# A finer table for placing masks, sums, reciprocals and products in the output stages of an attention and GEGLU kernel

## The chip, the cores and the metric

One core of a Trainium2 chip runs the whole program. The metric is the device time of one execution in microseconds, given as the median of several runs.

## What is computed

Sliding-window attention over 8 batches, 8 heads, 576 positions and 64 dimensions, then a feed-forward block with a gate. Heads 0 to 3 see the last 32 positions; heads 4 to 7 see 32 positions at distances of 4.

```python
rel = pos[:, None] - pos[None, :]
mask_plain = (rel >= 0) & (rel < 32)
mask_dil = (rel >= 0) & (rel < 128) & (rel % 4 == 0)
scores = where(masks, q @ k.T / sqrt(64), -1e9)
attn = softmax(scores)
x = (attn @ v).transpose(0, 2, 1, 3).reshape(4608, 512)
out = (gelu(x @ w_gate) * (x @ w_val)) @ w_out      # 512 -> 1536 -> 512, float32
```

## The kernel before

**Chunks and units.** The feed-forward part goes through nine chunks (`c`) of 512 tokens. The attention is cut into 32 units (`n`): a batch has four, `n // 4` is the batch; of each four the first two are plain (two heads each), the last two dilated. Unit 4b + i fills the i-th of the four tiles `xT` for batch b, which is the i-th quarter of the contraction in the first feed-forward product. A chunk of tokens so needs all units of its batches before it can finish its first products. Chunks 1 to 5 do the attention of later batches between their own feed-forward work.

**One chunk.** The entry products (`ffn1`, L533, and `ffn1_two`, L545, for the first two of the twelve column blocks) make gate and value in two PSUM banks; ScalarE takes the Gelu (L557) and VectorE multiplies (L558) into `u_all`. `ffn1_two` goes through the contraction quarter by quarter, so that the last unit's `xT` is needed only for its last four products of sixteen. Then the output products (`ffn2`, L564): four blocks of 128 tokens, twelve products each, every block stored by a copy on ScalarE (`store`, L575) and a DMA on SyncE's queue. This last part of a chunk is called its output stage.

**One attention unit.** Scores (`emit_s`, L339 plain, L369 dilated) go into the four banks `SB`; ScalarE takes the exponential into a tile `P` (L349 and L350, L371). What lies outside the window has to become zero. There are two ways. With `pe_mask` four products of the identity with a bias tile (L332 plain, L355 dilated) are put into PSUM ahead of the scores, so the exponential gives zero there. Otherwise VectorE multiplies `P` by a mask of zeros and ones (L379, called "mask" below). The list `biased` names the units that use the bias. Units 0 to 3 always do. Then `emit_pv` (L383; products at L442) makes the values ("num": P times v) and the sums ("den": P times ones). VectorE turns the sums into reciprocals with a transpose, a reciprocal and a transpose (`norm_r`: L500, L505, L507; "chain" below) and multiplies (`norm_x`: L518 plain, L521 dilated; "product" below) into `xT`. In chunks 3 to 6 some units are done during the entry products instead (`values_a`), in the scores' banks, with wider forms.

**The banks.** PSUM has eight banks. `mm0` is 0 or 4 and names the half that a chunk's feed-forward uses; `SB = 4 - mm0` is the scores' half. In the output stage of chunks 1 to 5, block 0 goes to a bank (`first`) of the last entry products, blocks 1 to 3 all go to bank `mm0`, and values and sums take the banks `V = mm0 + 1` to `mm0 + 3`. `first` is one of these. In a plain unit the values take bank V and 64 columns of the next, the sums the end of bank V + 1 and bank V + 2. The halves are swapped after chunks 1, 2 and 3.

**The order.** The program is emitted in the order of the text, and each engine keeps that order; the schedule is written by hand. In an output stage the table `places` says where what goes: "2.3s" means scores before the fourth product (number 3) of block 2, "1.12v" a unit's values after block 1, behind its store. In chunks 1 to 5 a "v" emits values, sums, the next waiting mask, the chain and the product together; in the last block the mask is left for later. One unit's scores are emitted during the last entry products of the chunk, so that its exponential can run beside block 0. The lines that the change and the prediction touch:

```python
        SB = 4 - mm0
...
        V = mm0 + 1
...
            first = pairs[(NNB - 2 + swap) % 2] + (pairs[(NNB - 2 + swap) % 2] == mm0)
```

Of the kernel before, what the change touches and what calls it, by code (L numbers as in the profile page):

```python
# [38 lines left out]
def kernel(  # L39
# [11 lines left out]
    B, H, S, D = q.shape  # L51
# [328 lines left out]

        return emit_mask

    def emit_pv(n, b0, parts=("num", "den"), wide=False):  # L383


        b, hp = n // NHP, n % 2
        vp, vd, vt, vr = tiles["v", b]
        pt = tiles["P", n]
        mms = []

        def add(hl, c0, dims, lhs, p0, pdims, st):

            base = ps[64 * hl : 64 * hl + 64, b0 + c0 // 512, c0 % 512 : c0 % 512 + 1]
            o = bass.AP(tensor=base.tensor, offset=base.offset, ap=[base.ap[0]] + dims)
            rhs = bass.AP(tensor=pt.tensor, offset=pt.offset + p0, ap=[pt.ap[0]] + pdims)
            mms.append((o, lhs, rhs, st))

        def run(n):
            return [[1, n]]

        if is_plain(n):
            if "num" in parts:
                for j in range(5):
                    for hl in range(2):
                        lhs = vp[:, j, hp, 2 * hl, :] if j < 4 else vt[:, hp, 2 * hl, :]
                        w = (PW, PW, PW, P, PT)[j]
                        add(hl, j * P, run(w), lhs, hl * PH + j * PW - (32 if j == 4 else 0), run(w), j in (0, 4))
            if "den" in parts:
                d0 = 1024 if wide else 960

                groups = (
                    ((0, 0, 4, P), (P, P, 3, 32), (PH - PT, 512, 1, PT))
                    if wide
                    else ((0, 0, 1, 64), (64, 64, 1, 64), (PW, P, 3, P), (P, P, 3, 32), (PH - PT, 512, 1, PT))
                )
                for i, (p0, q0, runs, w) in enumerate(groups):
                    for hl in range(2):
                        st = i == 0 or i == (2 if wide else 1)
                        add(hl, d0 + q0, [[P, runs], [1, w]], ones[:, 0:D], hl * PH + p0, [[PW, runs], [1, w]], st)
        else:  # L420
            if "num" in parts:
                for s in range(2):
                    for m in range(3):
                        for hl in range(2):
                            h, p0 = 2 * hp + hl, (2 * s + hl) * DW
                            if m < 2:
                                add(hl, 512 * s + m * NCL, run(P), vd[:, h, 2 * m + s, :], p0 + m * NCL, run(P), m == 0)
# [3 lines left out]
            if "den" in parts:  # L431

                groups = (
                    ((0, 0, DW, 1024), (1, 0, DW, 1536))
                    if wide
                    else ((0, 0, 192, 288), (0, 192, 96, 800), (1, 0, 96, 896), (1, 96, 192, 1312))
                )
                for i, (s, c, w, c0) in enumerate(groups):
                    for hl in range(2):
                        add(hl, c0, run(w), ones[:, 0:D], (2 * s + hl) * DW + c, run(w), wide or i != 2)  # L440
        for o, lhs, rhs, st in mms:
            nc.tensor.matmul(o, lhs, rhs, start=st, stop=True, skip_group_check=True)  # L442

# [236 lines left out]
    scores = {0: range(4, 8), 1: range(8, 12), 2: range(12, 17), 3: range(17, 22), 4: range(22, 27), 5: range(27, 32)}  # L680
    values_b = {1: range(8, 12), 2: range(12, 16), 3: range(17, 20), 4: range(22, 24), 5: range(27, 28)}
    values_a = {3: {4: 16}, 4: {2: 20, 6: 21}, 5: {1: 24, 4: 25, 7: 26}, 6: {1: 28, 4: 29, 7: 30, 10: 31}}
    biased = (6, 7, 8, 9, 10, 11, 12, 13, 14, 15)

    four = "1.5s 1.9v 1.12s 2.6v 2.12s 3.3v 3.12s 3.12v"
    three = "1.4s 1.12v 2.3s 2.12v 3.2s 3.12s 3.12v"
    two = "1.4s 1.12v 2.3s 2.12v 3.2s 3.12s"
    one = "1.4s 1.12v 2.3s 2.12s 3.6s"
    places = {1: four, 2: four, 3: three, 4: two, 5: one}
    places = {c: [(int(w[0]), int(w[2:-1]), w[-1]) for w in p.split()] for c, p in places.items()}  # L690
    late = None
    for c in range(NCH):
# [61 lines left out]
        if c == 0:  # L754
            load_batch_rest(2)
            ffn2(c, 0, 0, {5: [s_next]})
            store(c, 0, 0, "act")
            ffn2(c, 1, 1, {4: [s_next], 8: [lambda: md(4)]})
            store(c, 1, 1, "act")
            s_next()  # L760
            ffn2(c, 2, 0, {4: [lambda: md(5)], 6: [s_next], 9: [lambda: md(6)]})
            store(c, 2, 0, "act")
            ffn2(c, 3, 1, {2: [lambda: md(7), lambda: num(4, 4)], 8: [lambda: num(5, 6)]})
            store(c, 3, 1, "act")
            num(6, 2)
            num(7, 4)
        else:
            todo = list(values_b.get(c, ()))
            lone = c in values_b
            first = pairs[(NNB - 2 + swap) % 2] + (pairs[(NNB - 2 + swap) % 2] == mm0)  # L770

            def pv(last):
                n = todo.pop(0)
                emit_pv(n, V)
                if not last:
                    mask_next()
                norm(n, V)

            late = None
            mask_next()  # L780
            for tb in range(4):
                at = [(fc, kind) for t, fc, kind in places.get(c, ()) if t == tb]

                def do(kind, after):
                    if kind == "s":
                        s_next()
                        if not lone:
                            mask_next()
                    else:
                        pv(after and tb == 3)  # L790

                hooks = {}
                for fc, kind in at:
                    if fc < NNB:
                        hooks.setdefault(fc, []).append(lambda kind=kind: do(kind, False))
                bank = mm0 + tb if not lone else first if tb == 0 else mm0
                ffn2(c, tb, bank, hooks)
                store(c, tb, bank, "dve" if c > 5 and tb == 3 else "act")
                for fc, kind in at:
                    if fc == NNB:  # L800
                        do(kind, True)
            if lone:

                late = "bank"
                if len(values_b[c]) > 2:
                    mm0 = 4 - mm0
                    late = "x"
            while masks:
                mask_next()
# [28 lines left out]
```

The softmax here doesn't subtract the row's maximum and nothing guards it: scores larger than these inputs give would overflow.

## Time and profile before

| | |
|---|---|
| median of 5 runs | 362.01 us (361.17 to 362.93) |
| the profiled execution, its own time | 362.93 us |
| its span in the profile | 360.9 us |
| output stage of chunk 1: first output product to the end of the last | 91.3 to 107.2 us |
| chunk 2: first entry product, last four of `ffn1_two` | 109.0, 112.2 us |
| chunk 3: the same | 149.3, 152.5 us |
| VectorE: multiply of the Gelu (L558) | 108 of 683 ns |
| VectorE: transposes of the chain (L507) | 32 of 778 ns |
| ScalarE: table load between Gelu and exponential | 1.28 us |

The page of a profile gives busy time by engine and by groups of instructions: line, engine, operation, output and inputs with their shape, count, then busy time and mean length, then the idle time before the group and what ended it. The chain of waits gives start, length and what, in order of time, followed back from the last instruction. A timeline has start, length, engine, line and operation, and in brackets how long the engine was idle before and what released it. PE is TensorE, PEld its weight loads, DVE VectorE, ACT ScalarE, POOL GpSimd, SP SyncE. The lengths of single matmuls (380 ns at 512 columns) overlap; their distance is what counts.

### The profile page before, as it was taken

How to read it: one execution, taken by the hardware profiler on the slowest of the kernel's cores; microseconds unless marked ns; L12 is line 12 of the kernel's file. 1: busy time of each engine (PE TensorE's matmuls, PEld its weight loads, DVE VectorE, ACT ScalarE, POOL GpSimd, SP SyncE). 2: the span in 40 equal slices, each digit the busy share in tenths (PEclk: the TensorE clock that was granted, in tenths of full speed). 3: DMA queues.
4: the chain of work that ended last, by engine and by line, in shares of the span. 5: the costliest groups of instructions: out<-in, count | busy, mean ns of one | idle time of the engine just before them, and what ended most of it. 6: DMA issues, size and time to landing. Idle time of an engine off the chain costs nothing.

```text
span 360.9 us, 5997 instructions
## 1 busy us (share of the span) xinstructions
PE 344.7 (96%) x2358; PEld 166.3 (46%) x2358; DVE 196.1 (54%) x298; ACT 146.0 (40%) x212; POOL 78.2 (22%) x110
## 2 busy tenths in 40 slices
PE   5789999999989999899999999999999999999995
PEld 2554454444544445444444444544454444444442
DVE  3575446743275425765479838893679613403320
ACT  2733254253543354433663365436543223312321
POOL 2580344540431431044003410050000000000000
PEclk9959999999999999999999999999999999999999
DMA  8999999999999997599538961795100020011002
GB/s 201 235 179 211 218 142 203 176 164 238 185 130 229 181 157 126 136 170 145 112 94 187 157 96 74 181 161 84 60 29 0 13 105 2 1 61 57 0 29 87
DMA packets 107291, 45.30 MB, mean 126 GB/s; under 512 B 83040, under 2 KB 102496, under 8 KB 107264
## 3 DMA queue, kind: packets, MB, share of 16 engines
q1 hardware_dynamic: 84272, 31.21, 40.5%
q0 software_dynamic: 21456, 12.01, 26.5%
q10 hardware_dynamic: 1536, 1.70, 2.1%
q8 instruction: 18, 0.29, 0.4%
q14 instruction: 9, 0.07, 0.1%
HBM read 40.13 MB, written 9.44 MB: 137 GB/s over the span
## 4 chain that ended last, share of the span: by engine, by line
PE 79%; DMA 13%; DVE 4%; POOL 2%; ACT 1%; issue 0%; ACTq 0%; SPq 0%; POOLq 0%
PE ps L533 42%; PE ps L564 25%; PE ps L442 4%; DMA xT<-in_k_dram 3%; DMA st<-in_k_dram 3%; DMA wv<-in_moe_w_val_dram 3%; PE ps L545 3%; DMA wo<-in_moe_w_out_dram 2%; DVE xT L521 1%; PE ps L369 1%; DMA sv<-in_v_dram 1%; PE ps L339 1%; PE ps L455 1%; DVE dt L500 1%; DVE rb L507 1%; PE ps L355 1%
## 5 line engine op out<-in xcount | busy, mean ns | idle before, releaser
L558 DVE SCALAR_TENSOR_TENSOR u_all<-g,ps 128x512 f16<-128x512 f16 x108 | 72.6, 683 | 75.7 <-PE ps L533 66.0
L557 ACT ACTIVATE g<-ps 128x512 f16<-128x512 f32 x108 | 63.6, 597 | 123.5 <-PE ps L533 109.6
L564 PE MATMUL ps<-wo,u_all 128*128 128x512 f16 x432 | 101.1, 380 | 0.8 <-DMA wo<-in_moe_w_out_dram 0.4
L533 PE MATMUL ps<-xT,wg 128*128 128x512 f16 x392 | 100.6, 379 | 0.3
L533 PE MATMUL ps<-xT,wv 128*128 128x512 f16 x392 | 100.6, 379 | 0.0
L564 PEld LDWEIGHTS <-u_all 128*128 128x128 f16 x432 | 39.2, 98 | 45.1 <-issue 1.2
L533 PEld LDWEIGHTS <-wv 128*128 128x128 f16 x392 | 38.4, 98 | 46.4 <-issue 0.2
L533 PEld LDWEIGHTS <-wg 128*128 128x128 f16 x392 | 37.3, 98 | 44.6 <-issue 2.1
L575 ACT ACTIVATE osb<-ps 128x512 f32<-128x512 f32 x33 | 19.7, 597 | 48.6 <-PE ps L564 48.6
L500 DVE STREAM_TRANSPOSE dt<-ps 128x576 f32<-128x576 f32 x25 | 19.5, 779 | 26.2 <-PE ps L442 26.1
L199 POOL CAST qp<-st 128x2048 f16<-128x2048 f32 x6 | 11.4, 1893 | 100.4 <-DMA st<-in_k_dram 87.5
L507 DVE STREAM_TRANSPOSE rb<-rc 128x576 f32<-128x576 f32 x32 | 24.9, 778 | 1.1
L371 ACT ACTIVATE P<-ps 128x1152 f16<-128x1152 f32 x16 | 18.1, 1129 | 13.5 <-PE ps L369 13.5
L349 ACT ACTIVATE P<-ps 128x960 f16<-128x960 f32 x16 | 15.5, 970 | 9.5 <-PE ps L339 9.5
L521 DVE TENSOR_TENSOR xT<-ps,rb 128x576 f16<-128x576 f32 x16 | 17.8, 1122 | 0.3
L577 DVE TENSOR_SCALAR osb<-ps 128x512 f32<-128x512 f32 x3 | 2.1, 692 | 27.8 <-PE ps L564 27.8
L545 PE MATMUL ps<-xT,wg 128*128 128x512 f16 x40 | 15.8, 395 | 1.4 <-DVE xT L521 0.9
L545 PE MATMUL ps<-xT,wv 128*128 128x512 f16 x40 | 15.7, 392 | 0.0
L442 PE MATMUL ps<-P,ones 128*64 128x192 f16 (+5 forms) x174 | 11.6, 248 | 2.2 <-ACT P L371 1.0
L379 DVE TENSOR_TENSOR P<-P,mask_p 128x1344 f16<-128x1344 f16 x10 | 9.3, 938 | 6.8 <-ACT P L350 6.8
L379 DVE TENSOR_TENSOR P<-P,mask_d 128x1152 f16<-128x1152 f16 x8 | 6.1, 757 | 11.1 <-ACT P L371 11.1
L470 DVE STREAM_TRANSPOSE dt<-ps 64x576 f32<-64x576 f32 x14 | 10.9, 781 | 0.4
(83 smaller groups left out, 268.5 us busy)
## 6 DMA issues: line engine op xcount, KB each, us to landing
out_dram<-osb SPq DMA_DIRECT2D x36, 256.0 KB, 2.0
sv<-in_v_dram SPq DMA_DIRECT2D x40, 128.0 KB, 3.7
st<-in_q_dram SPq DMA_DIRECT2D x24, 128.0 KB, 3.6
st<-in_k_dram SPq DMA_DIRECT2D x24, 128.0 KB, 3.1
qd<-in_q_dram POOLq DMA_DIRECT2D x7, 256.0 KB, 4.6
qd<-in_k_dram POOLq DMA_DIRECT2D x7, 256.0 KB, 6.3
vd<-in_v_dram POOLq DMA_DIRECT2D x7, 256.0 KB, 7.3
wg<-in_moe_w_gate_dram POOLq DMA_DIRECT2D x3, 512.0 KB, 8.2
```

What stands on the lines that cost most here:

```text
L349: nc.scalar.activation(pt[:, :, 0:PB], sb[:, 0, :, 0:PB], AF.Exp, bias=0.0, scale=scale)
L371: nc.scalar.activation(pt, ps[:, b0 : b0 + 4, 0:DW], AF.Exp, bias=0.0, scale=scale)
L442: nc.tensor.matmul(o, lhs, rhs, start=st, stop=True, skip_group_check=True)
L500: nc.vector.transpose(dst, den)
L507: nc.vector.transpose(rb.rearrange("p (b c) -> p b c", c=32), bass.AP(tensor=rc.tensor, offset=rc.offset, ap=[rc.ap[0], [1, 18], [0, 32]]),)
L521: nc.vector.tensor_tensor(dst.rearrange("p (i m s) -> p i m s", m=2, s=2), num, rb.rearrange("p (s m i) -> p i m s", s=2, m=2), ALU.mult,)
L533: nc.tensor.matmul(ps[:, b0 + gi, :], w[:, kc, ns], xT[kc][:, tok], start=(kc == 0), stop=(kc == NKC - 1))
L545: nc.tensor.matmul(ps[:, pairs[nb] + gi, :], w[:, kc, ns], xT[kc][:, tok], start=(kc == 0), stop=(kc == NKC - 1),)
L557: nc.scalar.activation(g, ps[:, b0, :], AF.Gelu)
L558: nc.vector.scalar_tensor_tensor(u_all[:, nb, :], g, USCALE, ps[:, b0 + 1, :], ALU.mult, ALU.mult)
L564: nc.tensor.matmul(ps[:, bank, :], u_all[:, fc, tb * P : (tb + 1) * P], wo_t[fc // 4][:, fc % 4, :], start=(fc == 0), stop=(fc == NNB - 1),)
L575: nc.scalar.activation(osb, ps[:, bank, :], AF.Copy, bias=0.0, scale=1.0 / USCALE)
```

## The change

The table of places is rewritten with more kinds of entries: "v" emits sums, values and the chain; "x" the product; "m" a mask; "s" scores; "w" is a "v" in the scores' banks. Sums are emitted before values wherever both are emitted at once. The first unit's values of an output stage follow block 0 by two products in chunks 1 to 3. Units 8 to 15 lose the bias products and get masks on VectorE. In chunk 1 the last unit's values go to the scores' banks, and the halves of PSUM are not swapped afterwards; after chunks 2 and 3 they are.

```diff
-    def emit_pv(n, b0, parts=("num", "den"), wide=False):
+    def emit_pv(n, b0, parts=("den", "num"), wide=False):
...
-            if "num" in parts:
-                for j in range(5):
-                    for hl in range(2):
-                        lhs = vp[:, j, hp, 2 * hl, :] if j < 4 else vt[:, hp, 2 * hl, :]
-                        w = (PW, PW, PW, P, PT)[j]
-                        add(hl, j * P, run(w), lhs, hl * PH + j * PW - (32 if j == 4 else 0), run(w), j in (0, 4))
             if "den" in parts:
...
+            if "num" in parts:
+                for j in range(5):
+                    for hl in range(2):
+                        lhs = vp[:, j, hp, 2 * hl, :] if j < 4 else vt[:, hp, 2 * hl, :]
+                        w = (PW, PW, PW, P, PT)[j]
+                        add(hl, j * P, run(w), lhs, hl * PH + j * PW - (32 if j == 4 else 0), run(w), j in (0, 4))
...
-    biased = (6, 7, 8, 9, 10, 11, 12, 13, 14, 15)
-    four = "1.5s 1.9v 1.12s 2.6v 2.12s 3.3v 3.12s 3.12v"
-    three = "1.4s 1.12v 2.3s 2.12v 3.2s 3.12s 3.12v"
-    two = "1.4s 1.12v 2.3s 2.12v 3.2s 3.12s"
-    one = "1.4s 1.12v 2.3s 2.12s 3.6s"
-    places = {1: four, 2: four, 3: three, 4: two, 5: one}
+    biased = (6, 7)
+    places = {
+        1: "0.0m 1.2v 1.2x 1.2s 1.2m 1.12s 2.1v 2.1x 2.1m 2.12s 3.1v 3.1m 3.1x 3.12w 3.12x",
+        2: "0.0m 1.2v 1.2x 1.2s 1.2m 1.12s 2.1v 2.1x 2.1m 2.12s 3.1v 3.1x 3.1m 3.7s 3.12v 3.12x 3.12m",
+        3: "0.0m 1.2v 1.2x 1.2s 1.2m 1.12s 2.1v 2.1x 2.1m 2.12s 2.12m 3.1v 3.1x 3.7s 3.7m",
+        4: "0.0m 1.4s 1.12v 1.12x 1.12m 2.3s 2.12v 2.12x 2.12m 3.2s 3.2m 3.12s 3.12m",
+        5: "0.0m 1.4s 1.4m 1.12v 1.12x 2.3s 2.3m 2.12s 2.12m 3.6s 3.6m",
+    }
...
-            def pv(last):
-                n = todo.pop(0)
-                emit_pv(n, V)
-                if not last:
+            going = []
+            def do(kind):
+                if kind == "s":
+                    s_next()
+                elif kind == "m":
                     mask_next()
-                norm(n, V)
+                elif kind == "x":
+                    norm_x(*going.pop(0))
+                else:
+                    n, bank = todo.pop(0), SB if kind == "w" else V
+                    emit_pv(n, bank)
+                    norm_r(n, bank)
+                    going.append((n, bank))
             late = None
-            mask_next()
             for tb in range(4):
                 at = [(fc, kind) for t, fc, kind in places.get(c, ()) if t == tb]
-                def do(kind, after):
-                    if kind == "s":
-                        s_next()
-                        if not lone:
-                            mask_next()
-                    else:
-                        pv(after and tb == 3)
                 hooks = {}
                 for fc, kind in at:
                     if fc < NNB:
-                        hooks.setdefault(fc, []).append(lambda kind=kind: do(kind, False))
+                        hooks.setdefault(fc, []).append(lambda kind=kind: do(kind))
                 bank = mm0 + tb if not lone else first if tb == 0 else mm0
                 ffn2(c, tb, bank, hooks)
                 store(c, tb, bank, "dve" if c > 5 and tb == 3 else "act")
                 for fc, kind in at:
                     if fc == NNB:
-                        do(kind, True)
+                        do(kind)
             if lone:
                 late = "bank"
                 if len(values_b[c]) > 2:
-                    mm0 = 4 - mm0
                     late = "x"
+                    if c > 1:
+                        mm0 = 4 - mm0
             while masks:
                 mask_next()
```

In the dilated branch of `emit_pv` the two parts are exchanged in the same way.

More of the change, by code (lines that the diff above doesn't have):

```diff
@@ L419, in emit_pv @@
                         add(hl, d0 + q0, [[P, runs], [1, w]], ones[:, 0:D], hl * PH + p0, [[PW, runs], [1, w]], st)
-        else:
+            if "num" in parts:
[4 more added lines that the diff above has]
+                        add(hl, j * P, run(w), lhs, hl * PH + j * PW - (32 if j == 4 else 0), run(w), j in (0, 4))
+        else:
+            if "den" in parts:
+                groups = (
+                    ((0, 0, DW, 1024), (1, 0, DW, 1536))
+                    if wide
+                    else ((0, 0, 192, 288), (0, 192, 96, 800), (1, 0, 96, 896), (1, 96, 192, 1312))
+                )
+                for i, (s, c, w, c0) in enumerate(groups):
+                    for hl in range(2):
+                        add(hl, c0, run(w), ones[:, 0:D], (2 * s + hl) * DW + c, run(w), wide or i != 2)
             if "num" in parts:
@@ L430, in emit_pv @@
                                 add(hl, 512 * s + P, two, vr[:, h, s, :], p0 + P, two, False)
[L431 to L440, printed above, removed]
         for o, lhs, rhs, st in mms:
```

## The prediction

> **What bounds the kernel now.** I read the page's engine rows first, then the chain of waits for the output stage of chunk 1 (90 to 113 us), then timelines of single hand-overs. The page says that TensorE (PE) is the bound and that VectorE (DVE) has room on average:
>
> ```profile
> PE 344.7 (96%) x2358; PEld 166.3 (46%) x2358; DVE 196.1 (54%) x298; ACT 146.0 (40%) x212; POOL 78.2 (22%) x110
> ...
> L521 DVE TENSOR_TENSOR xT<-ps,rb 128x576 f16<-128x576 f32 x16 | 17.8, 1122 | 0.3
> ...
> L379 DVE TENSOR_TENSOR P<-P,mask_p 128x1344 f16<-128x1344 f16 x10 | 9.3, 938 | 6.8 <-ACT P L350 6.8
> L379 DVE TENSOR_TENSOR P<-P,mask_d 128x1152 f16<-128x1152 f16 x8 | 6.1, 757 | 11.1 <-ACT P L371 11.1
> ```
>
> The chain (start, length, what) shows what the change removes and what PE waits for:
>
> ```profile
> 90.36 0.57 PE ps L332 x4
> 90.93 0.40 PE ps L339 x10
> 91.33 3.78 PE ps L564 x17
> ...
> 98.51 0.49 PE ps L355 x4
> ...
> 105.20 0.80 DVE dt L500
> ...
> 107.13 1.14 DVE xT L521
> 108.27 0.04 issue
> 108.31 0.75 PE ps L442 x20
> ...
> 111.01 1.14 DVE xT L521
> 112.15 0.04 issue
> 112.19 1.02 PE ps L545 x4
> ```
>
> A plain unit's bias costs 0.57 us of PE, a dilated one's 0.49. Twice PE stands for VectorE: unit 11's values wait for unit 10's product (its nine output products would have ended at 107.03: 1.28 us idle), and the last quarter of the next stage's first products waits for unit 11's (0.6 us). Stage 2 repeats this at 147.46 to 152.51 (0.77 and 0.6 us). From chunk 6 on PE runs without a gap, and there the change touches nothing.
>
> Output blocks 1 to 3 share one PSUM bank, so a block must wait for the store copy of the block before. Where only scores stand between two blocks, the timeline of chunk 5 shows the price:
>
> ```profile
> 256.95 0.29 PE L369 MATMUL ps<-qTd 64*128 64x128 f16 x4
> ...
> 257.06 0.60 ACT L575 ACTIVATE osb<-ps 128x512 f32<-128x512 f32 x1 [0.70 <-PE ps L564]
> ...
> 257.71 0.81 PE L564 MATMUL ps<-wo,u_all 128*128 128x512 f16 x3 [0.32 <-ACT osb L575]
> ```
>
> From the end of a block to the start of the next are 0.76 us (0.11 to ScalarE, 0.60 copy, 0.05 back). Scores of 0.37 leave 0.39 idle, bias with scores (1.0) or sums with values (0.7) leave next to nothing.
>
> [...] 48 output products of chunk 6 take 10.36 us, 215.8 each. [...] One mask took 1.70 us beside a GpSimd cast that began just before it; most others take 0.86:
>
> ```profile
> 59.18 1.70 DVE L379 TENSOR_TENSOR P<-P,mask_p 128x1344 f16<-128x1344 f16 x1
> ```
>
> **The change part by part.** Prices from the timelines, in us. PE: output or entry product 0.216; switch from such products into scores or sums 0.10 (four products before one take 0.97, not 0.86); scores 0.40 plain, 0.37 dilated; sums with values 0.72 plain (sums 0.40 of it), 0.66 dilated (0.35). ScalarE: exp 1.35 plain, 1.13 dilated; store 0.60. VectorE: mask 0.86 and 0.76; reciprocal chain (transpose, reciprocal, transpose) 1.90; product 0.76 and 1.12. Hand-overs: PE to others 0.11, ScalarE to VectorE 0.04, either to PE 0.05.
>
> *Removed:* bias of units 8 to 15, 4 × 0.57 + 4 × 0.49 = 4.2 us of PE, all on the path. *Added:* eight masks, 4 × 0.86 + 4 × 0.76 = 6.5 us of VectorE. *Moved:* values of the first unit from ninth to second product of block 1; sums before values, so the chain starts 0.3 earlier; the mask of unit n+1 stands behind unit n's chain and product, which on VectorE's queue means that the next sums wait for all three. GpSimd's and SyncE's orders do not change; data for the earliest moved scores (unit 16) land at 137.84 and are wanted at about 142.8.
>
> Stage 1, forward from the trace. Gate products end at 90.19; switch and scores 8 follow, output products start at 90.69 (91.26 before). The exp is held by its table load, 91.44 to 92.79 as before; mask 8 ends 93.69. Block 0 ends 93.28, is stored by 93.99; sums 8 share its bank and start 94.04 instead of 93.81. Values end 94.76, scores 9 95.16, block 1 97.32. Scores 10 (97.42) cannot cover the store: block 2 starts 98.18 (0.39 idle). VectorE: chain 8 94.55 to 96.45, product 97.23, mask 9 98.12; sums 9 start 98.50, in time. Block 2 ends 101.59, scores 11, 0.39 idle again, block 3 from 102.45. Chain 9 ends 100.91, product 101.69, mask 10 102.48; sums 10 at 102.77. Chain 10 to 105.06, mask 11 105.85, product 10 106.93. Unit 11 goes to the scores' banks, so it needs only its mask: 105.90 to 106.56. Its chain queues behind product 10: 106.96 to 108.86, product 110.01. As the bank halves are not swapped after chunk 1, the next entry products wait 0.2 for product 10's bank and then 0.7 for product 11: last quarter at 110.06, where it was 112.19. Gain 2.1: bias 2.12, old waits 1.9, new ones 1.9.
>
> Stage 2. Chunk 2's remaining entry products start 1.06 after the last quarter, at 111.12, and take 17.26 as before, to 128.38; output products from 128.88. Exp 12 waits for its table load as before and mask 12 ends 131.88; sums 12 start 132.00 unhindered. Block 1 ends 135.28, mask 13 136.08, 0.39 idle, sums 13 136.46. Block 2 ends 139.55, mask 14 140.44, 0.39 idle, sums 14 140.73, scores 16 142.79, block 3 ends 144.27. On VectorE, chain 14 runs to 143.0, product 14 to 144.17, mask 15 to 144.96: PE, ready at 144.37, waits 0.64. Values 15 end 145.67, chain 147.3, product 148.45; last quarter at 148.50 (PE itself: 148.26), where it was 152.51. Gain 1.9, together 4.0: bias 2.12, old waits 1.4, new ones 1.7.
>
> Stage 3 loses no bias. Values no longer stand between blocks, so two store waits of 0.39 are new, and unit 20's mask, written before unit 19's chain, holds that chain for its exp (till 181.56); product 19 still ends at 184.6, before the last quarter at 186.1. Old waits of 0.87 go, 1.05 come: −0.2.
>
> Stage 4: mask 23 moves behind chain and product 22. It ends 0.3 after PE arrives at the sums (220.00 against 219.69, in times of before); 0.2 is left after the store wait. A mask less before the first entry product gives 0.1 back. Together −0.1. Stage 5 and the wide units of chunks 3 to 6: mask 28 moves by no instruction, and sums before values start a chain earlier that 20 to 40 entry products cover; the same waits end last; nothing.
>
> Sum: 2.1 + 1.9 − 0.2 − 0.1 = 3.7 us. The profiled execution spans 360.9 (362.93 with what lies around it); its copy would span 357.2. The median of five runs is 362.01, so I expect 358.3.
>
> *Unknown costs.* Whether the transpose starts when the sums end: if only after the values, 0.3 more in each of stages 1 and 2, 0.6 in all; I take nothing, since before it starts 0.11 after the last sums, and no other use lies between. Masks 9 and 13 fall beside GpSimd's DMA issues (97.3 to 99.3; 134.2 to 136.7): from nothing to 0.8 each, the excess of the mask above; I take nothing, as there the cast explains the wait. Store waits: 0 to 0.39 each, six of them; I take the measured one.
>
> **The rivals.** *Waits grow a little.* The two unknowns come true: gain 3.7 − 0.6 − 1.6 = 1.5, 360.5. For it: stages 1 and 2 hang on VectorE; against: the measured hand-overs. *New waits do not bind:* store waits and mask waits hide in places that I priced too high; the gain is the bias and half of the old waits, 4.2 + 1.3 = 5.5: 356.5. Against: the quoted 0.39. *VectorE's turn becomes the bound, slower:* sums, chain, product, mask, next sums is one ring; a dilated turn is 0.35 + 0.11 + 1.90 + 1.12 + 0.76 + 0.05 = 4.3 us, against PE's 4.0 for a block with scores, sums, values and store wait. Some eight turns hang on it. Each 0.1 more per turn costs 0.8; from 0.47 per turn the gain is gone; at 0.7 it would be 358.3 + 5.6 = 363.9. For it: VectorE's load in stages 1 and 2 grows from 11.6 and 11.8 us (busy in 90 to 112 and 130.5 to 152.5) by 3.2 each to some 15 out of 20. Against: every length in the ring is measured.
>
> **How the numbers follow.** Forecast 0.72, waits grow 0.15, nothing binds 0.07, slower ring 0.06. The likeliest is 358.3; alone it reaches 357.2 to 359.4. With the unknown costs the range is 356.7 to 360.7. This kernel's measurement tells 0.3% (1.1 us) from no change. Faster 0.90 (the first and third case and most of the second), same 0.05, slower 0.05.
>
> **What would show it.** No L332 or L355 products after 62 us but unit 6's and 7's; PE idle about 0.39 after the scores between blocks of chunks 1 to 3, ended by the store; the last quarter of L545 about 2.1, 4.0 and 3.8 us earlier in chunks 2, 3 and 4; PE waiting for masks before units 15 and 23. I am wrong if masks take clearly over 0.9, or transposes start after the values, or chunk 3's first products do not come 4 us earlier.

## The result and the profile after

| | median of its runs | ratio to before (95% interval) |
|---|---|---|
| before | 362.19 us (51 runs, 360.93 to 363.72) | |
| after | 360.48 us (30 runs, 359.16 to 361.77) | 0.9954 (0.9946 to 0.9962) |

The change saves 1.7 us where 3.7 were forecast. The profiled executions span 360.9 and 359.1 us. The time lies inside the predicted range, but over half of the expected gain is missing, and that is the question of this part.

Rows of the new kernel's profile that answer to those of before:

```profile
PE 343.1 (96%) x2326; PEld 165.7 (46%) x2326; DVE 201.6 (56%) x306; ACT 145.2 (40%) x212; POOL 78.3 (22%) x110
...
L564 PE MATMUL ps<-wo,u_all 128*128 128x512 f16 x432 | 100.9, 380 | 2.3 <-ACT osb L575 2.2
...
L379 DVE TENSOR_TENSOR P<-P,mask_p 128x1344 f16<-128x1344 f16 x14 | 11.8, 851 | 10.8 <-ACT P L350 10.8
...
L442 PE MATMUL ps<-P,ones 128*64 128x192 f16 (+5 forms) x174 | 12.2, 255 | 4.0 <-DVE P L379 1.9
...
L379 DVE TENSOR_TENSOR P<-P,mask_d 128x1152 f16<-128x1152 f16 x12 | 9.0, 750 | 5.5 <-ACT P L371 5.5
```

And of the kernel before:

```profile
L564 PE MATMUL ps<-wo,u_all 128*128 128x512 f16 x432 | 101.1, 380 | 0.8 <-DMA wo<-in_moe_w_out_dram 0.4 <-ACT osb L575 0.3
...
L442 PE MATMUL ps<-P,ones 128*64 128x192 f16 (+5 forms) x174 | 11.6, 248 | 2.2 <-ACT P L371 1.0 <-DVE P L379 0.8 <-ACT P L350 0.4
...
L442 PE MATMUL ps<-P,vd 128*64 128x128 f16 x128 | 7.3, 236 | 1.8 <-DVE xT L521 1.8
```

PE has 32 instructions less (eight units with four bias products each) and VectorE eight masks more. The last field of a row is the idle time before the group. It has grown before the output products: 0.8 us in all before, now 2.3, of which 2.2 for the store copy. Before sums and values together it is the same: 2.2 for the sums and 1.8 for the dilated values before, now 4.0 for the sums and nothing for the values, since the sums now come first. Only what PE waits for there has changed: the 1.8 for products of the unit before are gone, and the waits for masks have grown from 0.8 to 1.9. The masks themselves do not get longer on average (938 and 757 ns before).

The chain of waits in the output stage of chunk 1 (start, length, what):

```profile
93.67 0.61 ACT osb L575
...
97.80 0.61 ACT osb L575
...
102.07 0.61 ACT osb L575
...
103.09 0.66 PE ps L442 x20
...
103.78 0.80 DVE dt L500
...
105.60 0.72 DVE P L379
106.32 1.06 DVE xT L521
...
109.21 1.14 DVE xT L521
...
110.39 1.02 PE ps L545 x4
```

No bias is left. Three store copies stand on this chain of waits, and at its end VectorE: unit 10's reciprocal chain, mask 11, product 10, chain 11, product 11. The last quarter starts at 110.39 where it was 112.19 (forecast 110.06).

To see which stage gave what, I cut the trace of each kernel into chunks. Chunk 1 runs from its first entry product; it and chunks 2 and 3 end where the last quarter of the next chunk's first products ends; from chunk 4 on a chunk ends with the next one's first entry product. Lengths in us, from one profile each:

| | c1 | c2 | c3 | c4 | c5 | c6 | sum |
|---|---|---|---|---|---|---|---|
| before | 44.08 | 40.32 | 37.39 | 33.04 | 36.77 | 33.77 | 225.37 |
| after | 42.11 | 39.09 | 37.83 | 33.48 | 37.03 | 33.95 | 223.49 |
| gain | 1.97 | 1.23 | −0.44 | −0.44 | −0.26 | −0.18 | 1.88 |
| forecast gain | 2.1 | 1.9 | −0.2 | −0.1 | 0 | 0 | 3.7 |

Stage 1 came nearly as forecast; each later one fell short: 0.67, 0.24, 0.34, 0.26 and 0.18, together 1.7. Another execution of the same program (the first experiment) has chunks 2 to 6 the same within 0.01 us, so tenths can be read there. Chunk 1 is no such ruler: it differed by 0.2 between the two, and mask 9 took 1.05 us in the one and 0.85 in the other. Some expectations below count a chunk from first entry product to first entry product; on that count before has 39.80, 40.32, 37.85 and 36.86 for chunks 1 to 4, after 37.67, 39.23, 38.31 and 37.30. Where I compare with such a number I say so.

### The profile page after: what moved, and what is told of

Same layout as the page of the kernel before. It is cut to its first block, busy times and chain, and to the rows that moved or that the text cites. A ratio compares the mean times of both kernels' runs of the same rounds, so it can differ in the third digit from the quotient of the medians.

```text
span 359.1 us, 5943 instructions
## 1 busy us (share of the span) xinstructions
PE 343.1 (96%) x2326; PEld 165.7 (46%) x2326; DVE 201.6 (56%) x306; ACT 145.2 (40%) x212; POOL 78.3 (22%) x110
## 4 chain that ended last, share of the span: by engine, by line
PE 80%; DVE 10%; DMA 4%; ACT 3%; issue 2%; ACTq 0%; DVEq 0%
PE ps L533 42%; PE ps L564 24%; PE ps L442 5%; PE ps L545 4%; DMA xT<-in_k_dram 4%; DVE xT L521 2%; DVE dt L500 2%; DVE rb L507 1%; DVE dt L470 1%; PE ps L339 1%; ACT osb L575 1%; PE ps L369 1%; DVE u_all L558 1%; DVE xT L480 1%; PE ps L355 1%
## 5 line engine op out<-in xcount | busy, mean ns | idle before, releaser
L500 DVE STREAM_TRANSPOSE dt<-ps 128x576 f32<-128x576 f32 x25 | 19.5, 778 | 16.9 <-PE ps L442 16.9
L507 DVE STREAM_TRANSPOSE rb<-rc 128x576 f32<-128x576 f32 x32 | 24.9, 778 | 1.1
L521 DVE TENSOR_TENSOR xT<-ps,rb 128x576 f16<-128x576 f32 x16 | 17.9, 1128 | 0.3
L379 DVE TENSOR_TENSOR P<-P,mask_p 128x1344 f16<-128x1344 f16 x14 | 11.8, 851 | 10.8 <-ACT P L350 10.8
L577 DVE TENSOR_SCALAR osb<-ps 128x512 f32<-128x512 f32 x3 | 2.1, 691 | 27.8 <-PE ps L564 27.8
L442 PEld LDWEIGHTS <-ones 128*64 128x64 f16 x174 | 7.4, 112 | 14.6 <-issue 13.0
L379 DVE TENSOR_TENSOR P<-P,mask_d 128x1152 f16<-128x1152 f16 x12 | 9.0, 750 | 5.5 <-ACT P L371 5.5
```

The costliest lines, as they stand in the source:

```text
L379: nc.vector.tensor_tensor(pt, pt, mb, ALU.mult)
L500: nc.vector.transpose(dst, den)
L507: nc.vector.transpose(rb.rearrange("p (b c) -> p b c", c=32), bass.AP(tensor=rc.tensor, offset=rc.offset, ap=[rc.ap[0], [1, 18], [0, 32]]),)
L521: nc.vector.tensor_tensor(dst.rearrange("p (i m s) -> p i m s", m=2, s=2), num, rb.rearrange("p (s m i) -> p i m s", s=2, m=2), ALU.mult,)
```

## The experiments

Every kernel was timed in five rounds beside the kernel before. An interval is 0.1 to 0.2% wide to each side, up to 0.6 us, so a verdict on a few tenths rests on the chunk lengths.

**v_first: the order of sums and values, by the argument.** An edit that did not do what it was meant to.

```diff
-    def emit_pv(n, b0, parts=("den", "num"), wide=False):
+    def emit_pv(n, b0, parts=("num", "den"), wide=False):
```

> The new kernel with values before sums everywhere, as in the kernel before. Theory (sums first brings nothing in the output stages, because the transpose waits for the unit's last values product, which shares a bank with the sums; and it costs in the wide units 26 and 30, whose sums lie in the banks that the unit before frees last): the idle 0.46 us ahead of unit 26's and 0.3 us ahead of unit 30's products go, the rest stays; 0.7 us under the new kernel, about 359.8. Rival (sums first lets the chain start early, and other things ate the gain): 0.6 to 1 us above the new kernel, about 361.3.

360.68 us, 0.9955 (0.9937 to 0.9973). `parts` is only asked with "in"; the order of the text decides. The program is that of the changed kernel, and the run is a repeat. It says nothing on the order.

**v_first_wide: values before sums in the wide units alone.**

```diff
-                    emit_pv(pend, SB, wide=True)
+                    emit_pv(pend, SB, ("num",), wide=True)
+                    emit_pv(pend, SB, ("den",), wide=True)
```

> The new kernel with values before sums in the wide units alone; in the output stages sums stay first. Theory: the same as with values first everywhere, 0.7 us under the new kernel, about 359.8; the two differ by less than 0.3 us. Rival: this one is better than values first everywhere by 0.6 us or more.

360.22 us, 0.9938 (0.9922 to 0.9954). Chunks 5 and 6 are back at 36.77 and 33.77, the lengths of before to the hundredth; nothing else moves but chunk 1 (42.81). The timeline of unit 26 (chunk 5) in the new kernel:

```profile
235.74 1.51 DVE L480 TENSOR_TENSOR xT<-ps,rb 64x576 f16<-64x576 f32 x2
...
237.31 0.44 PE L442 MATMUL ps<-P,ones 128*64 128x288 f16 x4 [0.30 <-DVE xT L480]
```

And with values first:

```profile
236.14 1.53 DVE L480 TENSOR_TENSOR xT<-ps,rb 64x576 f16<-64x576 f32 x2
...
237.33 0.30 PE L442 MATMUL ps<-P,vd 128*64 128x128 f16 x4
...
237.72 0.44 PE L442 MATMUL ps<-P,ones 128*64 128x288 f16 x4
```

Two products of the unit before (L480, shown as one row of two) free the scores' banks. The sums go to banks 2 and 3 of them, which the second product of the pair frees: they start 0.06 after its end, PE idle 0.30 before. The values' first bank is free earlier: they start 0.34 before the pair ends, with no wait. So sums first costs 0.26 in chunk 5 and 0.18 in chunk 6 (unit 30).

**bias_only and table_only: each half of the change by itself.** The kernel before with masks instead of bias for units 8 to 15, and the new kernel with the bias kept.

```diff
 # bias_only, in the kernel before
-    biased = (6, 7, 8, 9, 10, 11, 12, 13, 14, 15)
+    biased = (6, 7)
 # table_only, in the kernel after
-    biased = (6, 7)
+    biased = (6, 7, 8, 9, 10, 11, 12, 13, 14, 15)
```

> The kernel before with the bias taken from units 8 to 15 and nothing else. Theory (4.2 us of PE's work go, but masks put the chain of units 10, 11, 14, 15 behind exponentials, and scores alone no longer cover the store's copy): about 0.8 us are left in each of stages 1 and 2, 360.4 to 361.0. Rival one (the bias is worth its 4.2 us and the new table takes some of it away): under 359. Rival two (only the table makes it worth anything): 362 or more.

> The new kernel with the bias kept for units 8 to 15; the entries for their masks then do nothing. Theory: PE's 4.2 us come back, 1.6 of them cover store waits, and unit 15's wait of 1 us for its mask goes; 1.7 us above the new kernel, about 362.1, no gain over the kernel before. Rival (the table brings the gain, by unit 11's own banks and earlier values): clearly under the kernel before, 361 or less.

bias_only: 360.73 us, 0.995 (0.9936 to 0.9964). table_only: 362.42 us, 1.0005 (0.9996 to 1.0015). Taking the bias away alone brings as much as the whole change, by one-profile lengths 0.62 in chunk 1 and 0.73 in chunk 2. The table alone brings nothing in sum: chunks 1 and 2 gain 0.77 and 0.41, and chunks 3 to 6 lose 0.43, 0.45, 0.26 and 0.18, the same as in the new kernel. So the losses of chunks 3 to 6 belong to the table and the order, not to the bias. In chunks 1 and 2 the two parts help each other: 3.20 together, 1.35 and 1.18 apart, though the tenths of chunk 1 are not safe.

**values_first: sums after values in every unit.**

```diff
+        sums = [m for m in mms if m[1].tensor is ones.tensor]
+        mms = [m for m in mms if m[1].tensor is not ones.tensor] + sums
         for o, lhs, rhs, st in mms:
```

> Values really before sums everywhere (the run called v_first swapped only the default of an argument; the order of the text decides, so it was the new kernel once more). Theory: the waits of units 26 and 30 in chunks 5 and 6 go (0.26 and 0.18 us of these chunks, as with values first in the wide units alone); in chunks 1 to 4 nothing changes, since the transpose waits for the last product of the unit either way: about 0.45 us under the new kernel, 360.1. Rival (the sums' place in the narrow units matters): chunks 2 to 4 grow by 0.2 us or more each.

359.81 us, 0.9943 (0.9926 to 0.996). Chunks 5 and 6 are again those of before. Chunk 4 stays at 33.51 (33.48 with sums first): in that chunk the order inside a unit makes no difference, so there sums first starts no chain earlier. The chunk lost its 0.44 to something else. Chunks 2 and 3 get longer, by 0.31 and 0.33 (39.55 and 38.62 on the other count): there sums first does help, for another reason. The first unit follows block 0 by two products, its values begin in bank V, and in chunks 2 and 3 that is the bank `first` which block 0's store copy still reads. Sums, which lie elsewhere, fill that wait. The timeline of unit 12 in chunk 2 shows it (L577 is the store copy, L444 the products of `emit_pv`):

```profile
132.29 0.46 PE L444 MATMUL ps<-P,vp 128*64 128x160 f16 x8 [0.25 <-ACT osb L577]
```

Unit 17 in chunk 3 has the same 0.25. In chunk 1 `first` is bank V + 1, where a plain unit's sums begin, and it is the other way round: there the sums wait 0.25 in the new kernel, and values first wait for nothing.

**own_trigger: a chain that needs only the sums' banks.** The products that share a bank with the sums come first, then the sums, then the values of the other bank.

```diff
+            if "num" in parts:
+                values((0, 1) if wide else (1,))
             if "den" in parts:
...
-                    else ((0, 0, 192, 288), (0, 192, 96, 800), (1, 0, 96, 896), (1, 96, 192, 1312))
+                    else ((0, 0, 224, 800), (0, 224, 64, 1024), (1, 0, 288, 1088))
...
+            if "num" in parts and not wide:
+                values((0,))
...
-            c0, dims = (1024, [[512, 2], [1, 288]]) if wide else (288, [[512, 3], [1, 192]])
+            c0, dims = (1024, [[512, 2], [1, 288]]) if wide else (800, [[1, S]])
```

This is the dilated branch; in the plain one the values with j = 4 come first.

> New kernel with the values that share a bank with the sums first, then the sums, then the other values, and a dilated unit's sums placed in two banks instead of three; in the wide units values first. The last product into the sums' banks is then a sum, so the transpose can start before the unit's last values. Theory (chains that start 0.3 us late are what stages 2 to 4 lost against the forecast): each chain starts 0.15 to 0.25 us before its unit ends on TensorE; chunk 2 gets shorter by 0.4 to 0.7, chunks 3 and 4 by 0.2 each, chunks 5 and 6 by 0.45 together: 358.9 to 359.4. Rival (the ring of VectorE is not what ends these stages): only chunks 5 and 6 gain, 360.1.

359.87 us, 0.9938 (0.9924 to 0.9952). The reason for it stands in the timeline of unit 8 in the new kernel:

```profile
94.31 0.49 PE L442 MATMUL ps<-P,ones 128*64 128x64 f16 x10 [0.25 <-ACT osb L575]
...
94.61 0.46 PE L442 MATMUL ps<-P,vp 128*64 128x160 f16 x8
...
94.88 0.22 PE L442 MATMUL ps<-P,vt 128*64 128x64 f16 x2
...
95.21 0.78 DVE L500 STREAM_TRANSPOSE dt<-ps 128x576 f32<-128x576 f32 x1 [1.35 <-PE ps L442]
```

The sums are over at 94.80, the transpose starts at 95.21: 0.11 after the last values product, the hand-over that I had measured, but after another instruction. Those values lie in a bank that the transpose reads. The same unit in own_trigger (L453 is `emit_pv`, L511 the first transpose of the chain):

```profile
93.67 0.49 PE L453 MATMUL ps<-P,ones 128*64 128x64 f16 x10
...
93.97 0.46 PE L453 MATMUL ps<-P,vp 128*64 128x160 f16 x8
...
94.28 0.78 DVE L511 STREAM_TRANSPOSE dt<-ps 128x576 f32<-128x576 f32 x1 [1.08 <-PE ps L453]
```

Now the chain starts 0.11 after the last sum and 0.15 before the last values product, which goes to a bank that the transpose does not read, is over. Wherever VectorE is free, own_trigger's narrow units behave so: the chain starts 0.04 to 0.11 after the last sum and 0.08 to 0.23 before the values end. It is the last product into the transpose's banks that counts, neither the sums alone nor the end of the unit. Whether the program's semaphores or the banks themselves ask for this, no run here shows. The dilated chain 15 starts 0.62 after the start of its unit, 0.77 in the new kernel. Chunks 3 and 4 gain 0.09 each (37.74 and 33.39; on the other count 38.51, which holds chunk 2's late unit too, and 37.20), chunks 5 and 6 are those of before. Chunk 2 gains nothing (39.29 for 39.09; 39.17 on the other count), against expectation, and the median lies above the expected range. VectorE's timeline shows where:

```profile
146.79 0.78 DVE L518 STREAM_TRANSPOSE rb<-rc 128x576 f32<-128x576 f32 x1
...
148.04 1.12 DVE L532 TENSOR_TENSOR xT<-ps,rb 128x576 f16<-128x576 f32 x1 [0.47 <-DVE rb L518]
```

Product 15 stands still for 0.47 us behind a chain that is done, with TensorE's values finished long before (145.76; in this kernel L511, L518 and L532 are the L500, L507 and L521 of the new one). The same product has the same 0.47 in best_of. The trace shows no cause, and I have none.

**mask23_early: unit 23's mask ahead of unit 22's chain.** Nothing but chunk 4's table.

```diff
-        4: "0.0m 1.4s 1.12v 1.12x 1.12m 2.3s 2.12v 2.12x 2.12m 3.2s 3.2m 3.12s 3.12m",
+        4: "0.0m 1.4s 1.12m 1.12v 1.12x 2.3s 2.12m 2.12v 2.12x 3.2s 3.2m 3.12s 3.12m",
```

> New kernel with chunk 4's masks of the next unit written before the chain, as in the kernel before, where they were behind chain and product. Theory: the 0.76 us for which the sums of unit 23 wait for their mask go, of which the store's copy keeps 0.1 to 0.3: chunk 4 gets back to the 36.86 us of before (37.30 in the new kernel), 0.45 us under the new kernel, 360.1. Rival (chunk 4 lost to something else): no change, 360.5.

359.68 us, 0.9938 (0.992 to 0.9956); chunk 4 goes from 33.48 to 32.91 (36.73 on the other count), under the 33.04 of before. The timeline of units 22 and 23 in the new kernel:

```profile
213.03 0.44 PE L442 MATMUL ps<-P,ones 128*64 128x192 f16 x8
...
213.86 0.78 DVE L500 STREAM_TRANSPOSE dt<-ps 128x576 f32<-128x576 f32 x1 [3.89 <-PE ps L442]
...
215.79 1.13 DVE L521 TENSOR_TENSOR xT<-ps,rb 128x576 f16<-128x576 f32 x1
...
216.84 0.75 DVE L379 TENSOR_TENSOR P<-P,mask_d 128x1152 f16<-128x1152 f16 x1
...
217.64 0.44 PE L442 MATMUL ps<-P,ones 128*64 128x192 f16 x8 [0.60 <-DVE P L379]
```

And with the mask ahead:

```profile
211.74 0.76 DVE L379 TENSOR_TENSOR P<-P,mask_d 128x1152 f16<-128x1152 f16 x1 [2.50 <-ACT P L371]
...
213.05 0.78 DVE L500 STREAM_TRANSPOSE dt<-ps 128x576 f32<-128x576 f32 x1 [0.55 <-PE ps L442]
...
214.98 1.14 DVE L521 TENSOR_TENSOR xT<-ps,rb 128x576 f16<-128x576 f32 x1
...
216.24 0.44 PE L442 MATMUL ps<-P,ones 128*64 128x192 f16 x8
```

Above, VectorE stood idle 3.89 us before the chain while the mask's input was there, and then sums 23 wait for the mask behind chain and product: nine output products from 214.93 at 0.216 are through at 216.88, so PE loses 0.76 (the bracket has less, as it counts from modelled ends). Below, the mask fits into that idle time, and the sums wait for nothing.

**best_of: own_trigger with better tables for chunks 3 and 4.** Chunk 4 as just shown; in chunk 3 the masks go ahead of the chains too, and the values go back between the blocks, where the kernel before has them.

```diff
-        3: "0.0m 1.2v 1.2x 1.2s 1.2m 1.12s 2.1v 2.1x 2.1m 2.12s 2.12m 3.1v 3.1x 3.7s 3.7m",
+        3: "0.0m 1.4s 1.12m 1.12v 1.12x 2.3s 2.12m 2.12v 2.12x 3.2s 3.12s 3.12v 3.12x",
```

> The own-trigger order, with chunks 3 and 4 placed as in the kernel before (values between the blocks, masks ahead of the chain) and chunks 1 and 2 as in the new kernel. Theory: chunk 3 gets back to 37.85 or under (38.31 in the new kernel), chunk 4 to 36.86, chunks 5 and 6 to 36.77 and 33.77, chunks 1 and 2 gain 0.6 more: 3.4 us under the kernel before, about 358.7. Rival (the parts don't add up, since a stage's start shifts what VectorE does): 360 or more.

358.6 us, 0.9915 (0.9896 to 0.9933). Chunks 3 to 6 are 37.39, 32.96, 36.77 and 33.77: what the new table lost there is back (on the other count chunks 1 to 4 have 38.79, 39.18, 38.16 and 36.78). Chunk 1 is 43.27 in this profile, 1.2 longer than after, because mask 9 took 2.23 us, as the timeline of GpSimd and VectorE shows:

```profile
95.58 0.61 POOL L200 CAST qp<-st 64x512 f16<-64x512 f32 x1
...
96.14 0.77 POOL L213 DMA_DIRECT2D vd<-in_v_dram  x1
...
96.26 2.23 DVE L379 TENSOR_TENSOR P<-P,mask_p 128x1344 f16<-128x1344 f16 x1
...
96.89 1.25 POOL L218 DMA_DIRECT2D vr<-in_v_dram  x2
...
98.10 1.28 POOL L183 CAST vp<-sv 128x1024 f16<-128x1024 f32 x1
```

The casts of queries and keys had ended when the mask began, and until 98.10 GpSimd only issued DMAs. This is no single case. In nine profiles of this kernel and its variants mask 9 begins beside these DMA issues with no cast running. It takes 0.85 to 0.88 us in three (the new kernel, last_wide, best2), and 1.05, 1.29, 1.34, 1.50, 1.53 and 2.23 in six (v_first, own_trigger, values_first, dil_bias, v_first_wide, best_of).

**dil_bias: the bias kept for the dilated units 10, 11, 14 and 15.** This takes the masks out of VectorE's ring, and nothing else.

```diff
-    biased = (6, 7)
+    biased = (6, 7, 10, 11, 14, 15)
```

> New kernel with the bias kept for the dilated units 10, 11, 14 and 15 alone. Theory (the ring sums, chain, product, mask, next sums on VectorE ends stages 1 and 2): a dilated turn loses its mask of 0.76 us, while the bias costs TensorE almost nothing, since bias and scores (0.96 us) lie where TensorE otherwise waits for the store's copy. Chunk 2's wait of 1.0 us before unit 15 and the one of 0.6 us before the last quarter shrink by about 0.7 and 0.6: chunk 2 from 39.23 to about 38.2, chunk 1 shorter by 0.3 to 0.5; 359.1. Rival (TensorE's own work ends these stages): four bias groups come back, 0.4 to 2 us slower than the new kernel, 361 or more.

359.97 us, 0.9941 (0.9927 to 0.9955). Chunk 2 goes from 39.09 to 38.67 (38.63 on the other count). PE's wait before unit 15 falls from 1.00 to 0.35, now for the product (`[0.18 <-DVE xT L521]`), and the bias costs 0.21 instead of its 0.49, since it fills the store wait: 0.96 lie between the blocks (140.01 to 140.97) instead of 0.75. I had expected about 1.0; 0.42 came. The wait before unit 15 fell by 0.65, as product 14 now ends last where the mask did, and 0.21 of that went to the bias. The wait before the last quarter of the next first products, which was to go too, stayed (0.48 in both timelines): chain and product 15 follow unit 15 as before. Chunk 1 was 42.60 with mask 9 at 1.50 us (38.33 on the other count), which hides what stage 1 gained.

**best2, best3: the parts together.** best2 is best_of with dil_bias; best3 keeps the bias of unit 9 as well, to take mask 9 away from GpSimd.

```diff
 # best2
-    biased = (6, 7)
+    biased = (6, 7, 10, 11, 14, 15)
 # best3
+    biased = (6, 7, 9, 10, 11, 14, 15)
```

> The combination best_of with the bias kept for units 10, 11, 14 and 15. Theory: what that bias saves in chunks 1 and 2 adds to best_of's gain: about 1.3 us under it, 357.8; chunks 3 to 6 as in best_of (38.16, 36.78, 36.77, 33.77). Rival: 359 or more.

> As best2, with the bias kept for unit 9 as well. Unit 9's mask falls into GpSimd's loads and casts for batch 3 and took from 0.85 to 2.23 us in the profiles so far, and chunk 1 from 37.67 to 38.79. Theory (GpSimd holds that mask): TensorE pays 0.57 us, chunk 1 no longer depends on GpSimd and takes 37.6 to 38.0; in the median within 0.4 us of best2. Rival (the mask's length has another cause): chunk 1 varies as before.

best2: 358.28 us, 0.9893 (0.9879 to 0.9906), the fastest, 3.9 us under before and 2.2 under the new kernel by medians. Its chunks: 41.97, 38.49, 37.39, 32.96, 36.77, 33.77. Of the 1.3 us expected under best_of, 0.3 came in the median. best3: 358.46 us, 0.9902 (0.9886 to 0.9918); chunk 1 42.63, on the other count 38.47 where 37.6 to 38.0 was expected. The interval does not part the two, so best3 does not tell what mask 9 costs in the median.

**v_loads_early: does GpSimd hold mask 9?** The DMA issues of the dilated values go ahead of the casts of queries and keys.

```diff
-        qp = cast_qk_plain(b, st)
         load_v_dil(b)
+        qp = cast_qk_plain(b, st)
         v_cast(b, sv)
```

> New kernel with GpSimd's three loads of the dilated heads' values written ahead of its casts of queries and keys, so that they are issued some 14 us earlier in chunk 1 and do not lie beside mask 9. Theory: mask 9 waits only for a cast that is running when it comes, 1.1 us at most and mostly less: 0.86 to 1.3 us, chunk 1 within 37.6 to 38.2. If the mask takes 1.3 us or more with no cast beside it, the cause is another. In the median 0 to 0.5 us under the new kernel.

361.32 us, 0.9974 (0.9962 to 0.9985): slower than the new kernel by some 0.8 us, and mask 9 longer, not shorter. A miss as a remedy, but the timeline shows a cast running when the mask starts:

```profile
96.79 1.89 POOL L199 CAST qp<-st 128x2048 f16<-128x2048 f32 x1 [15.36 <-DMA st<-in_k_dram]
...
97.06 2.34 DVE L379 TENSOR_TENSOR P<-P,mask_p 128x1344 f16<-128x1344 f16 x1
98.62 1.24 POOL L200 CAST qp<-st 64x512 f16<-64x512 f32 x1
```

The cast waits for its data and starts at 96.79, where it is 93.47 in the new kernel, so it begins 0.27 ahead of the mask. The mask ends 0.72 after the cast, almost a mask's length; the second cast, which takes 0.61 in the new kernel and in best_of, takes 1.24 beside it. That the mask waits at most 1.1 us was the author's estimate: here it took 1.49 more than in the new kernel. Chunk 1 is 1.48 longer (43.59; 39.16 on the other count), the excess of the mask (1.49).

**last_wide and best4: an earlier chain 15.** Unit 15 takes the wide form, whose sums have banks of their own. What was left open: whether the late start of the chain is worth what the sum of stage 2 lacks.

```diff
-        2: "0.0m 1.2v 1.2x 1.2s 1.2m 1.12s 2.1v 2.1x 2.1m 2.12s 3.1v 3.1x 3.1m 3.7s 3.12v 3.12x 3.12m",
+        2: "0.0m 1.2v 1.2x 1.2s 1.2m 1.12s 2.1v 2.1x 2.1m 2.12s 3.1v 3.1x 3.1m 3.7s 3.12u 3.12x 3.12m",
...
-                    n, bank = todo.pop(0), SB if kind == "w" else V
-                    emit_pv(n, bank)
-                    norm_r(n, bank)
+                    n, bank = todo.pop(0), {"w": SB, "u": mm0}.get(kind, V)
+                    emit_pv(n, bank, wide=kind == "u")
+                    norm_r(n, bank, wide=kind == "u")
```

> New kernel with unit 15, the last of chunk 2's output stage, in the wide form on the banks from mm0 on, sums first: its sums then have banks of their own, and the chain can start when the sums end. Theory (a chain that starts 0.3 us late is half of what chunk 2 lost against the forecast): chain 15 starts within 0.5 us of the start of the sums instead of 0.8, and the wait of 0.63 us before the last quarter of chunk 3's first products shrinks by 0.3: chunk 2 (to the end of those products) from 39.09 to about 38.8, the rest unchanged. Rival (the product waits for something else): no change.

> The combination best2 with unit 15 in the same wide form. Theory: chunk 2 from 38.49 to about 38.2, 0.2 to 0.4 us under best2, 357.9 to 358.1. Rival: no change against best2.

last_wide: 360.46 us, 0.9946 (0.9931 to 0.9962). Its timeline:

```profile
145.18 0.44 PE L442 MATMUL ps<-P,ones 128*64 128x288 f16 x4 [0.84 <-DVE P L379]
...
145.65 0.78 DVE L500 STREAM_TRANSPOSE dt<-ps 128x576 f32<-128x576 f32 x1 [0.53 <-PE ps L442]
...
147.68 1.13 DVE L521 TENSOR_TENSOR xT<-ps,rb 128x576 f16<-128x576 f32 x1
...
148.87 0.38 PE L545 MATMUL ps<-xT,wg 128*128 128x512 f16 x1 [0.28 <-DVE xT L521]
```

The chain starts 0.47 after the start of the sums, 0.30 sooner than in the new kernel, and the last quarter comes 0.21 sooner in chunk 2 (38.88). The tenth between is lost ahead of the product, which starts 0.13 after the chain instead of 0.04. best4, best2 with the same edit: 358.67 us, 0.9898 (0.9881 to 0.9915), chunk 2 38.37 for 38.49, where 0.2 to 0.4 under best2 was expected; the intervals don't tell it from best2.

## Why the prediction was right in its signs and wrong in its size

- **The bias and the stores: right.** 32 products went, and six new store waits cost about 0.38 each (scores with the wait 0.75, without 0.37). PE waits for masks before units 15 and 23, as named. The last quarters of the first products came 1.80, 3.03 and 2.59 us earlier in chunks 2, 3 and 4, where 2.1, 4.0 and 3.8 were forecast.
- **"Whether the transpose starts when the sums end … I take nothing": this step failed.** The transpose starts after the unit's last values product, 0.04 to 0.12 us after it. I had taken the 0.11 from the old order, in which the sums are last, which can't tell "after the sums" from "after the last product in these banks"; the new code, whose last values share a bank with the sums, tells them apart. A dilated chain so starts 0.76 after the start of its sums, where the forecast's times have 0.38. Of the difference 0.30 is the late start, the size that the prediction itself had named for this case. The other 0.08 is a slip in its times: its own prices, 0.35 for the sums and 0.11 for the hand-over, make 0.46, and last_wide, with the sums in banks of their own, has 0.47. Shown: own_trigger, whose chains start before the unit's last values end; values_first, where chunk 4 doesn't care for the order. What it costs is shown in part: in last_wide and own_trigger an earlier chain brought 0.21 of 0.30, and 0.09 of 0.15 in each of chunks 3 and 4. "I am wrong if … transposes start after the values, or chunk 3's first products do not come 4 us earlier" named both signs, and both came.
- **Stage 1: right in its sum, with luck.** It gained 1.97 of 2.1, but the late chain is there too: chain 10 starts 0.76 after its sums start, and the forecast's times have 0.39. What follows was shorter than priced. From the end of chain 10 to the last quarter 5.00 us were forecast (105.06 to 110.06) and 4.71 came (105.68 to 110.39), as mask, product and chain each start 0.08 before the end of the one ahead of them on VectorE. Two errors nearly cancel.
- **The late chain also came at more places than "0.6 in all" allowed for.** *Stage 2* kept my times up to the start of sums 14 (141.06, forecast 140.73, and the same 0.33 was there when the stage began). Then chain 14 is 0.38 later than its forecast distance, and chain 15 again, together 0.76:

```profile
141.06 0.44 PE L442 MATMUL ps<-P,ones 128*64 128x192 f16 x8
...
141.81 0.78 DVE L500 STREAM_TRANSPOSE dt<-ps 128x576 f32<-128x576 f32 x1 [0.83 <-PE ps L442]
...
145.60 0.44 PE L442 MATMUL ps<-P,ones 128*64 128x192 f16 x8 [0.84 <-DVE P L379]
...
146.37 0.78 DVE L500 STREAM_TRANSPOSE dt<-ps 128x576 f32<-128x576 f32 x1 [0.83 <-PE ps L442]
```

Overlapping masks and products give 0.1 of it back. That is the missing 0.67. *Stage 3*: chain 18 starts 0.76 after the start of its sums, and PE waits 0.45 for mask 19, a wait that the prediction does not list. *Stage 4*: mask 23 was to end 0.3 after PE's arrival; it was 0.76, and 0.38 of the difference is again chain 22. In stages 3 and 4 I had not asked what a late chain does to the mask behind it. mask23_early shows that mask's place costs 0.57. For the two links of stage 2 apart, one was tried (last_wide); the one from unit 14 to 15 rests on the timeline's arithmetic.
- **"Stage 5 and the wide units … nothing": failed.** That a wait for the unit before ends last there holds, but for the sums the second product of the pair ends it, for the values only the first. It costs 0.26 and 0.18, shown by v_first_wide to the hundredth. The 0.18 lies in chunk 6, so "From chunk 6 on … the change touches nothing" was wrong too.
- **"Masks 9 and 13 … I take nothing": right for 13 (0.85 or 0.86 in every profile that has it), not for 9.** It took 0.85 in the profile after, but between 0.85 and 2.34 elsewhere, and among the kernels with the same stage 1 chunk 1 grew with it, from 42.1 to 43.6. "There the cast explains the wait" is too narrow: six of the nine profiles in which mask 9 began beside DMA issues alone show 1.05 to 2.23. The other three show 0.85 to 0.88 (in best2 a mask of 0.85 us lay wholly beside the same issues). Spans on GpSimd are rough, so this is a sign only; why the mask took longer was not shown.
- **The rivals.** "Waits grow a little" gave 360.5, and 360.48 came, but only half by its way, so the agreement is luck. The late chain is its first unknown, in more places than it had; its second, both masks held, did not happen in the profile after. The wide units and mask 23 filled the sum instead. "New waits do not bind" falls with the store waits. Of "VectorE's turn becomes the bound" the ring was real: chain, product, mask and next sums decide stages 2 to 4, with 0.38 more per dilated turn than the forecast's times had. But PE waits for a mask at four places in the profile after, not eight, and the 0.47 each that it needed did not come.

## What to carry to other kernels

If an edit is to start a reader earlier by moving a producer forward, look at every writer of the banks that the reader takes: here it waited for the last one, 0.3 us after the one that was moved. In both timelines of mask23_early VectorE ran chain, product and mask in the order of the text; there a mask whose input was ready, put ahead of a longer chain that still waited for its own, made the chunk 0.57 us shorter. A wait that spare products fill at less than their price can be worth keeping, as the bias between blocks was (0.21 for 0.49). And try each part of a combined change alone, chunk by chunk: here the list `biased` alone brought as much as the whole, while the table won about 1.9 more in chunks 1 and 2 and gave 1.3 back in chunks 3 to 6.

## What the runs showed of the hardware that was not expected

- A mask of 0.85 us took 2.34 beside a GpSimd cast that began 0.27 before it (v_loads_early). Begun beside GpSimd's DMA issues with no cast running, it took 1.05 to 2.23 in six profiles and 0.85 to 0.88 in three. Why it took longer in some executions and not in others stays open.
- Where VectorE was free, the transpose of the sums started 0.04 to 0.12 us after the last TensorE product into the banks that it reads, whatever columns that product wrote (the new kernel, own_trigger, last_wide).
- In own_trigger, where the last values end after the chain has begun, most products start 0.10 to 0.20 after the chain; in the new kernel most start 0.04 after it. The cause is not shown.
- One product, unit 15's, stood 0.47 us with nothing left to wait for in the trace, in own_trigger and in best_of alike; in best2, best3 and best4 it starts 0.10 to 0.13 after its chain. Not explained, and not tried further.
